# Head pairs transposed together, half-batch loads and a hand-ordered merge in causal attention followed by a SwiGLU feed-forward

## The chip, the cores and the metric

The kernel runs on one core of one Trainium2 chip. The metric is the device time of one execution in microseconds (us). TensorE (PE) multiplies matrices, VectorE (DVE) and ScalarE (ACT) do elementwise work and read the accumulators in PSUM, GpSimd (POOL) does elementwise work in SBUF alone, and SyncE (SP) issues DMAs. Each engine runs its instructions in order and waits on semaphores for the others.

## What is computed

```python
# q, k, v: (8, 8, 576, 64); s: (8, 8, 576)
scores = q @ k.T / 8
cum = np.cumsum(np.maximum(s, 0), axis=-1)
bias = -(cum[..., :, None] - cum[..., None, :])
scores = np.where(causal, -1e9, scores + np.minimum(bias, 0))
attn = softmax(scores) @ v
x = attn.transpose(0, 2, 1, 3).reshape(4608, 512)   # rows: batch, position
g = x @ w_gate                                      # 512 x 1536
out = (g * sigmoid(g) * (x @ w_val)) @ w_out        # 1536 x 512
```

There are 64 heads of 576 positions and 64 dimensions. Inputs and output are float32; both kernels multiply in bf16.

## The kernel before

**Setup.** The running sum of `s` is made for all 64 heads at once by ten shifted additions on DVE (L97 to L103), split into a high and a low bf16 part, and turned by small PE transposes (L124 to L133), so that each head has four extra columns. Appended to the 64 dimensions of q and k, these four columns make the score matmul add the bias.

**Attention.** `load_group` (L135) reads q, k and v of four heads in 15 DMAs whose rows are 256 bytes. `do_head` (L186) casts q and k of one head to bf16 next to the extra columns, turns them with ten PE transposes of 128 columns (L202, five for k and five for q) into `KT` and `QT`, and copies each from PSUM (L205). Scores are made transposed in seven matmuls of 1,920 columns together (L221, the list `SCORE_CHUNKS`), ACT takes the exponential into `Pt` (L230), DVE multiplies each of the five diagonal blocks with a triangle (L239), and fifteen matmuls of 65 columns (L247) give the output and, in the last column, the sum by which L259 divides. The result goes to the DRAM scratch `xdr`.

**Feed-forward.** A tile (`do_moe_tile`, L278) is 512 rows of x. Four DMA transposes (L282) bring it from `xdr`; then for each of 12 column blocks there are four matmuls for the gate `pg` (L292) and four for the value `pv` (L300), a tanh on ACT (L308) and two DVE operations (L310, L314), which give `ht`. 48 matmuls (L320) make the output, ACT or DVE copies it and SP writes it. There are nine tiles.

**Order.** The program names heads, weight pieces and tiles one after another (L333 to L353): after a batch's eight heads come the tiles whose rows earlier batches have finished. A scheduler then orders each engine's instructions, so that in the trace the matmuls of heads and tiles alternate. Pieces of the weights are loaded between groups of heads (`load_weight_piece`, L168) in float32 and cast.

Of the kernel before, what the change touches and what calls it, by code (L numbers as in the profile page):

```python
# [12 lines left out]
FP32 = mybir.dt.float32  # L13
# [6 lines left out]
def kernel(  # L20
# [11 lines left out]
    nc = tc.nc  # L32

    B, H, S, D = q.shape
    BH = B * H
    NT, DM = out.shape
    DF = moe_w_gate.shape[1]

    SP = 640
    NCH = 5  # L40
    AUG = 4
    DEXT = D + AUG
    HGRP = 4

    PT_OFF = []
    o = 0
    for tj in range(NCH):
        PT_OFF.append(o)
        o += SP - 128 * tj
    PT_TOT = o  # L50

    SCORE_CHUNKS = [
        [(0, 0, 512)],
        [(0, 512, 640), (1, 128, 512)],
        [(1, 512, 640), (2, 256, 640)],
        [(3, 384, 640), (4, 512, 640)],
    ]

    const = ctx.enter_context(tc.tile_pool(name="const", bufs=1))
    prep = ctx.enter_context(tc.tile_pool(name="prep", bufs=1))  # L60
    stage = ctx.enter_context(tc.tile_pool(name="stage", bufs=2))
    head = ctx.enter_context(tc.tile_pool(name="head", bufs=4))
    small = ctx.enter_context(tc.tile_pool(name="small", bufs=4))
    wpool = ctx.enter_context(tc.tile_pool(name="wpool", bufs=1))
    moes = ctx.enter_context(tc.tile_pool(name="moes", bufs=4))
    hpool = ctx.enter_context(tc.tile_pool(name="hpool", bufs=3))
    xtp = ctx.enter_context(tc.tile_pool(name="xtp", bufs=8))

    apsum = ctx.enter_context(tc.tile_pool(name="apsum", bufs=1, space=bass.MemoryType.PSUM))
    mpsum = ctx.enter_context(tc.tile_pool(name="mpsum", bufs=4, space=bass.MemoryType.PSUM))  # L70

    dram = ctx.enter_context(tc.tile_pool(name="dram", bufs=1, space=bass.MemoryType.DRAM))

    ident = const.tile([128, 128], BF16)
    make_identity(nc, ident)
    keepmask = const.tile([128, 128], BF16)
    make_upper_triangular(nc, keepmask, val=1.0, diag=True)

    NPT = 4
    ptk_tiles = [const.tile([128, NCH, 128], BF16, name=f"ptk{i}") for i in range(NPT)]  # L80
    ptq_tiles = [const.tile([128, NCH, 128], BF16, name=f"ptq{i}") for i in range(NPT)]
    for t in ptk_tiles + ptq_tiles:
        nc.vector.memset(t[:, :, DEXT:128], 0.0)

    spos = prep.tile([BH, SP], FP32)
    nc.vector.memset(spos[:, S:SP], 0.0)
    s_sb = prep.tile([BH, S], FP32)
    nc.sync.dma_start(s_sb, s.flatten_outer_dims())
# [295 lines left out]
```

## Time and profile before

| | |
|---|---|
| median of 3 runs | 506.57 us (505.91 to 507.78) |
| the profiled execution | span 506.3 us |
| PE busy | 442.4 us (87%), 3,364 matmuls |
| DVE, ACT, POOL busy | 319.3, 298.2, 53.2 us |
[...]
| DMA | 57.44 MB, 46.7% of 16 engines' span |

The span is the time from the first to the last instruction of the profiled execution. "Busy" of an engine counts the time in which at least one of its instructions runs. Matmuls overlap in the pipeline, so a busy PE does not say how many columns it streams: the pace is read from the distance between starts.

### The profile page before, as it was taken

Reading aid. Unit: us, or ns where it says so; the run is one execution under the profiler, and the core shown is the slowest. Engines: PE = TensorE matmul, PEld = TensorE weight load, DVE = VectorE, ACT = ScalarE, POOL = GpSimd, SP = SyncE. Lnnn points to the kernel's source line nnn. Section 1 sums busy time; section 2 is a strip of 40 time slices with the busy share of each in tenths; the row PEclk is TensorE's granted clock in tenths of the full one; section 3 lists DMA queues with packets and bytes.
Section 4 is the critical chain, followed back from the end, with each engine's and each line's share of the span. In section 5 each row is a group of like instructions: output and inputs, shape, how many; then the busy total and the mean of one; then the engine's idle time right before and its main releaser. Section 6 shows DMA issues by size and latency. Waiting matters only on the chain.

```text
span 506.3 us, 10025 instructions
## 1 busy us (share of the span) xinstructions
PE 442.4 (87%) x3364; PEld 237.4 (47%) x3364; DVE 319.3 (63%) x991; ACT 298.2 (59%) x665; POOL 53.2 (11%) x248
## 2 busy tenths in 40 slices
PE   0277743658999999999999999999999999999997
PEld 0144532433445445554555465546554664444443
DVE  8348853645919846983798278828881887174570
ACT  3568865765439527972796289628952984232331
POOL 2013211110001101210121012102100100000000
PEclk9999985969999999999999999999999999999999
DMA  7805779677756751466255715671641121401102
GB/s 167 245 13 123 197 237 170 175 166 182 171 145 144 150 135 49 99 128 161 69 115 126 179 41 116 135 169 41 131 86 65 34 45 34 124 0 37 48 1 83
DMA packets 181124, 57.44 MB, mean 113 GB/s; under 512 B 173840, under 2 KB 173840, under 8 KB 181072
## 3 DMA queue, kind: packets, MB, share of 16 engines
q1 hardware_dynamic: 181072, 56.80, 46.7%
q8 instruction: 26, 0.43, 0.4%
q14 instruction: 26, 0.21, 0.1%
HBM read 37.90 MB, written 14.16 MB: 103 GB/s over the span
## 4 chain that ended last, share of the span: by engine, by line
PE 70%; DMA 10%; ACT 9%; DVE 4%; SPq 4%; issue 2%; ACTq 0%; POOL 0%; DVEq 0%; POOLq 0%
PE py L320 18%; PE pg L292 17%; PE pv L300 16%; PE sc L221 9%; PE tps L202 5%; PE av L247 5%; ACT Pt L230 4%; DMA wld<-in_moe_w_val_dram 3%; DMA wld<-in_moe_w_out_dram 2%; SPq L143 2%; DMA stgq<-in_q_dram 2%; ACT QT L205 1%; DMA stgtq<-in_q_dram 1%; DMA stgk<-in_k_dram 1%; PE htp L127 1%
## 5 line engine op out<-in xcount | busy, mean ns | idle before, releaser
L230 ACT ACTIVATE Pt<-sc 128x512 bf16<-128x512 f32 (+1 forms) x256 | 133.6, 581 | 14.4 <-PE sc L221 12.7
L292 PE MATMUL pg<-xt,wg 128*128 128x512 bf16 x432 | 123.6, 379 | 2.0 <-DMA xt<-xdr 1.5
L300 PE MATMUL pv<-xt,wv 128*128 128x512 bf16 x432 | 120.9, 379 | 0.0
L308 ACT ACTIVATE th<-pg 128x512 bf16<-128x512 f32 x108 | 65.0, 602 | 74.2 <-PE pg L292 69.2
L221 PE MATMUL sc<-QT,KT 128*128 128x128 bf16 (+3 forms) x448 | 87.5, 285 | 11.1 <-ACT QT L205 3.7
L310 DVE SCALAR_TENSOR_TENSOR pp<-th,pg 128x512 bf16<-128x512 bf16 x108 | 73.7, 683 | 35.9 <-ACT th L308 35.5
L320 PE MATMUL py<-wo,ht 128*128 128x512 bf16 x432 | 94.7, 379 | 0.0
L314 DVE TENSOR_TENSOR ht<-pp,pv 128x512 bf16<-128x512 bf16 x108 | 74.1, 686 | 7.8 <-PE pg L292 0.5
L239 DVE TENSOR_TENSOR Pt<-Pt,keepmask 128x128 bf16<-128x128 bf16 x320 | 64.5, 221 | 16.5 <-ACT Pt L230 14.5
L247 PE MATMUL av<-VT,Pt 128*128 128x65 bf16 x960 | 67.9, 198 | 6.9 <-DVE Pt L239 5.5
L328 ACT COPY ysb<-py 128x512 f32<-128x512 f32 x36 | 21.1, 586 | 79.8 <-PE py L320 75.0
L247 PEld LDWEIGHTS <-Pt 128*128 128x128 bf16 x960 | 48.6, 99 | 38.8 <-DVE Pt L239 30.5
L320 PEld LDWEIGHTS <-ht 128*128 128x128 bf16 x432 | 42.2, 98 | 51.0
L221 PEld LDWEIGHTS <-KT 128*128 128x128 bf16 x448 | 42.0, 98 | 50.3 <-issue 34.4
L300 PEld LDWEIGHTS <-wv 128*128 128x128 bf16 x432 | 40.4, 98 | 37.1 <-issue 2.6
L292 PEld LDWEIGHTS <-wg 128*128 128x128 bf16 x432 | 40.7, 98 | 34.9 <-issue 0.9
L197 DVE CAST ptk<-stgk 128x256 bf16<-128x256 f32 x45 | 12.7, 289 | 53.9 <-PE tps L202 48.6
L202 PE MATMUL tps<-ident,ptk 128*128 128x128 bf16 x320 | 31.3, 227 | 13.9 <-ACT ptk L197 13.5
L202 PE MATMUL tps<-ident,ptq 128*128 128x128 bf16 x320 | 35.3, 226 | 2.6 <-ACT KT L205 1.6
L202 PEld LDWEIGHTS <-ptk 128*128 128x128 bf16 x320 | 24.5, 101 | 20.2 <-ACT ptk L197 13.8
L205 DVE COPY KT<-tps 128x640 bf16<-128x640 bf16 x49 | 23.8, 487 | 13.5 <-PE tps L202 13.1
L259 DVE TENSOR_TENSOR ot<-av,recip 128x320 bf16<-128x320 f32 x64 | 31.1, 486 | 0.7 <-DVE Pt L239 0.3
(65 smaller groups left out, 277.2 us busy)
## 6 DMA issues: line engine op xcount, KB each, us to landing
out_dram<-ysb SPq DMA_DIRECT2D x36, 256.0 KB, 2.1
stgq<-in_q_dram SPq DMA_DIRECT2D x64, 128.0 KB, 3.0
stgk<-in_k_dram SPq DMA_DIRECT2D x64, 128.0 KB, 2.9
stgv<-in_v_dram SPq DMA_DIRECT2D x64, 128.0 KB, 2.8
xdr<-ot SPq DMA_DIRECT2D x64, 64.0 KB, 2.3
wld<-in_moe_w_gate_dram SPq DMA_DIRECT2D x4, 768.0 KB, 5.7
wld<-in_moe_w_val_dram SPq DMA_DIRECT2D x4, 768.0 KB, 6.6
wld<-in_moe_w_out_dram SPq DMA_DIRECT2D x12, 256.0 KB, 3.0
```

The source lines that it names most:

```text
L202: nc.tensor.transpose(tps[:, c * 128 : (c + 1) * 128], pt[:, c, :], ident)
L221: nc.tensor.matmul(sc[:, off : off + w], KT[:, 128 * tj : 128 * (tj + 1)], QT[:, ilo:ihi], start=True, stop=True,)
L230: nc.scalar.activation(Pt[:, pt_lo : pt_lo + width], sc[:, 0:width], AF.Exp, scale=0.125,)
L239: nc.vector.tensor_mul(Pt[:, o : o + 128], Pt[:, o : o + 128], keepmask)
L247: nc.tensor.matmul(av[:, bi * (D + 1) : (bi + 1) * (D + 1)], Pt[:, colo : colo + 128], VT[:, tj, :], start=(tj == 0), stop=(tj == bi),)
L259: nc.vector.tensor_mul(ot, av3[:, :, 0:D], recip[:, :, None].to_broadcast([128, NCH, D]),)
L292: nc.tensor.matmul(pg, WG[c][:, ft * 128 : (ft + 1) * 128], xts[c], start=(c == 0), stop=(c == 3),)
L300: nc.tensor.matmul(pv, WV[c][:, ft * 128 : (ft + 1) * 128], xts[c], start=(c == 0), stop=(c == 3),)
L308: nc.scalar.activation(th, pg, AF.Tanh, scale=0.5)
L310: nc.vector.scalar_tensor_tensor(pp, in0=th, scalar=1.0, in1=pg, op0=ALU.add, op1=ALU.mult)
L314: nc.vector.tensor_mul(ht, pp, pv)
L320: nc.tensor.matmul(py, hts[ft][:, ts_ * 128 : (ts_ + 1) * 128], WO[ft], start=(ft == 0), stop=(ft == 11),)
```

## The change

The kernel is written anew around the same arithmetic; the order on every engine is now the order in which the program names the instructions (`manual_schedule`).

- **Loads.** `load_qk` reads q or k of four heads (a half batch) in one DMA with rows of 1,536 bytes (96 partitions of six consecutive positions). `load_v` reads v of a whole batch in five DMAs.
- **Head pairs.** `cast_one` puts two heads side by side in 128 columns. For half batches 0 and 1 `pe_transpose` turns them on PE, six transposes for two heads. From half batch 2 on, `scratch` writes the casted rows to DRAM, `transposes` brings them back with one DMA transpose of 1,152 x 128 for k and one for q, and `split` copies the two 64-row halves on DVE into four standing tiles, whose other rows hold the bias columns (`aug`, a small DMA for each of the four tiles) or zeros (`init_x`).
- **Scores.** Nine matmuls of 1,600 columns together. The four full diagonal blocks are one chunk, which POOL masks with one `affine_select`.
- **First tile.** x of tile 0 is turned on PE out of SBUF (`x_pe`); the others come with one DMA transpose of 512 x 512 (`x_load`) after POOL has issued the write of a whole batch (`x_write`).
- **Merge.** `attn_items` and `ffn_items` yield after each small piece. `pump` advances attention up to a position, in heads; a tile has 36 items, over which eight heads are spread, with fixed offsets (`start`, `LAG`). The weight loads are hooked into it at eight places; their casts are DVE instructions at that place. All weights share two staging buffers.

```diff
-            tps = apsum.tile([128, SP], BF16, tag="tp", bufs=1, name="tps")
-            for c in range(NCH):
-                nc.tensor.transpose(
-                    tps[:, c * 128 : (c + 1) * 128], pt[:, c, :], ident
-                )
-            nc.any.tensor_copy(dstT, tps)
...
-            nc.vector.tensor_mul(
-                Pt[:, o : o + 128], Pt[:, o : o + 128], keepmask
-            )
...
-            next_stg = load_group((gi + 1) // GPB, (gi + 1) % GPB)
-        for h in range(g * HGRP, (g + 1) * HGRP):
-            do_head(b, h, stg)
-        nw = 1 if gi == 0 else 3
-        for _ in range(nw):
-            if wpiece < NWPIECE:
-                load_weight_piece(wpiece)
-                wpiece += 1
-        if g == GPB - 1:
-            while (moe_done + 1) * TT <= b * S:
-                do_moe_tile(moe_done)
-                moe_done += 1
...
+    CHUNKS = [
+        [(0, 0, 128), (1, 128, 256), (2, 256, 384), (3, 384, 512)],
+        [(0, 128, 576), (3, 512, 576)],
+        [(1, 256, 576), (2, 384, 576)],
+        [(4, 512, 576)],
+    ]
...
+    scp = ctx.enter_context(tc.tile_pool(name="scp", bufs=3, space=PSUM))
+    avp = ctx.enter_context(tc.tile_pool(name="avp", bufs=1, space=PSUM))
+    mp = ctx.enter_context(tc.tile_pool(name="mp", bufs=4, space=PSUM))
...
+    with tc.manual_schedule():
...
+        def load_qk(hb):
+            b, g = divmod(hb, 2)
+            for name, src in (("k", k), ("q", q)):
+                t = raw.tile([NP, HB, J, D], FP32, tag="raw" + name, name="raw" + name)
+                nc.sync.dma_start(
+                    t,
+                    src[b, g * HB : (g + 1) * HB, :, :].rearrange(
+                        "h (p j) d -> p h (j d)", j=J
+                    ),
+                )
+                loaded[name, hb] = t
...
+        def init_x(i, eng):
+            for T in (KX[i], QX[i]):
+                eng.memset(T[0][64:128, :], 0.0)
+                eng.memset(T[0][64:68, :], 1.0)
+                eng.memset(T[1][0:64, :], 0.0)
+                eng.memset(T[1][0:4, :], 1.0)
+            for e in range(2):
+                eng.memset(KX[i][e][64 * e : 64 * e + 64, NR * S :], 0.0)
+
+        init_x(0, nc.gpsimd)
...
+        def aug(hb, eng):
+            for T, k0 in ((KX, 0), (QX, 2)):
+                for e in range(2):
+                    r0 = 64 * (1 - e) + k0
+                    eng.dma_start(
+                        T[hb % 2][e][r0 : r0 + 2, 0 : NR * S].rearrange(
+                            "a (r s) -> a r s", r=NR
+                        ),
+                        AUG[hb * HB : (hb + 1) * HB, k0 : k0 + 2, :].rearrange(
+                            "(r e) a s -> e a r s", e=2
+                        )[e],
+                    )
...
+        def cast_one(hb, name, r, eng):
+            if r == 0:
+                cts[name, hb] = cp.tile([NP, NR, J, 2, D], BF16, tag="c" + name, bufs=1, name="c" + name)
+            eng.tensor_copy(
+                cts[name, hb][:, r].rearrange("p j e d -> p e j d"),
+                loaded[name, hb][:, 2 * r : 2 * r + 2, :, :],
+            )
...
+        def scratch(hb):
+            for name, SC in (("k", KS), ("q", QS)):
+                nc.sync.dma_start(
+                    SC[hb].rearrange("(r p j) c -> p r (j c)", r=NR, j=J),
+                    cts[name, hb].rearrange("p r j e d -> p r (j e d)"),
+                )
...
+        def transposes(hb):
+            for name, SC in (("k", KS), ("q", QS)):
+                prs[name, hb] = cp.tile([128, NR * S], BF16, tag="p" + name, bufs=1, name="p" + name)
+                nc.sync.dma_start_transpose(prs[name, hb], SC[hb])
+
+        def split(hb, name, eng):
+            T = {"k": KX, "q": QX}[name][hb % 2]
+            for e in range(2):
+                eng.tensor_copy(
+                    T[e][64 * e : 64 * e + 64, 0 : NR * S],
+                    prs[name, hb][64 * e : 64 * e + 64, :],
+                )
...
+            for j in range(J):
+                nc.tensor.transpose(
+                    ps[:, j, :], ct[:, r, j].rearrange("p e d -> p (e d)"), ident[0:NP, 0:NP]
+                )
...
+            if ci == 0:
+                nc.gpsimd.affine_select(
+                    pt[:, 1088:1600], pt[:, 1088:1600], pattern=[[0, 4], [1, 128]],
+                    compare_op=ALU.is_ge, fill=zreg, base=0, channel_multiplier=-1,
+                )
...
+        def x_write(b):
+            ot = ots[b]
+            nc.gpsimd.dma_start(xdr[b * S + 512 : (b + 1) * S, :], ot[0:TAIL, 4, :])
+            if b > 0:
+                nc.gpsimd.dma_start(
+                    xdr[b * S : b * S + 512, :].rearrange("(c p) e -> p c e", p=128),
+                    ot[:, 0:4, :],
+                )
+
+        def x_load(tt):
+            xts[tt] = xtp.tile([128, 4, TT], BF16, tag="xt", name="xt")
+            nc.sync.dma_start_transpose(xts[tt], xdr[tt * TT : (tt + 1) * TT, :])
...
+                nc.tensor.transpose(
+                    ps[:, c * 128 : (c + 1) * 128],
+                    ots[0][:, c, r * 128 : (r + 1) * 128],
+                    ident,
+                )
+            nc.vector.tensor_copy(xts[0][:, r, :], ps)
...
+            if hb + 1 < NHB:
+                if step == 0:
+                    aug(hb + 1, nc.sync)
+                    if hb + 2 < NHB:
+                        load_qk(hb + 2)
+                    cast_one(hb + 1, "k", 0, nc.gpsimd)
+                    cast_one(hb + 1, "k", 1, nc.gpsimd)
+                if step == 1:
+                    cast_one(hb + 1, "q", 0, nc.gpsimd)
+                    cast_one(hb + 1, "q", 1, nc.gpsimd)
+                    scratch(hb + 1)
+                    if hb % 2 == 0 and hb + 2 < NHB and hb > 0:
+                        load_v((hb + 2) // 2)
+                if step == 2:
+                    transposes(hb + 1)
+                    if hb % 2 == 1:
+                        for c in (0, 1):
+                            cast_v((hb + 1) // 2, c, nc.gpsimd)
+                if step == 3:
+                    split(hb + 1, "k", nc.vector)
+                    split(hb + 1, "q", nc.vector)
+                    if hb % 2 == 1:
+                        for c in (2, 3, 4):
+                            cast_v((hb + 1) // 2, c, nc.gpsimd)
...
+        def attn_items():
+            for bh in range(BH + 2):
+                if bh < BH:
+                    for ci in range(4):
+                        score_piece(bh, ci)
+                        if ci == 1:
+                            side(bh // HB, bh % HB)
+                        yield bh + ci / 8
+                p = bh - 1
+                if 0 <= p < BH:
+                    av_piece(p, (0, 1, 2))
+                    yield bh + 0.5
+                    av_piece(p, (3,))
+                    yield bh + 0.65
+                    av_piece(p, (4,))
+                    av_out(p)
+                    if p % H == H - 1:
+                        x_write(p // H)
+                    if p < H and p % 2 == 0 and p > 0:
+                        x_pe(p // 2 - 1)
+                    yield bh + 0.8
+                    if p == H - 1:
+                        x_pe(3)
+                if bh > H + 1 and (bh - 2) % H == H - 1:
+                    x_load((bh - 2) // H)
+                    yield bh + 0.9
...
+            for ft in range(NFT):
+                j, f0 = divmod(ft * 128, WCH)
+                pg = mp.tile([128, TT], FP32, tag="m", name="pg")
...
+        for nm in ("k", "q"):
+            cast_one(0, nm, 0, nc.vector)
+            cast_one(0, nm, 1, nc.vector)
+        aug(0, nc.scalar)
+        for nm in ("k", "q"):
+            pe_transpose(0, nm, 0, (nc.vector, nc.scalar))
+        for nm in ("k", "q"):
+            pe_transpose(0, nm, 1, (nc.vector, nc.vector))
+        nc.gpsimd.memset(VT[0][:, :, :, D : D + 1], 1.0)
+        nc.gpsimd.memset(VT[0][64:128, 4, :, 0:D], 0.0)
+        for c in range(5):
+            cast_v(0, c, nc.gpsimd)
+        init_x(1, nc.gpsimd)
+        aug(1, nc.sync)
+        nc.gpsimd.memset(VT[1][:, :, :, D : D + 1], 1.0)
+        nc.gpsimd.memset(VT[1][64:128, 4, :, 0:D], 0.0)
...
+        wq = [lambda j=j: load_wgv(j) for j in range(NWCH)] + [
+            lambda j=j: load_wo(j) for j in range(4)
+        ]
+        start = H + 1.2
+        for i in range(8):
+            pump(start * (i + 1) / 8)
+            if i % 2 == 1:
+                wq.pop(0)()
+        for tt in range(NTT):
+            lo = start if tt == 0 else H * (tt + 1) + LAG
+            hi = min(H * (tt + 2) + LAG, BH + 1)
+            span = 36 if tt < 6 else 25
+            n = 0
+            for _ in ffn_items(tt):
+                n += 1
+                pump(lo + (hi - lo) * min(1.0, n / span))
+                if wq and n % 5 == 1:
+                    wq.pop(0)()
+                if tt == NTT - 2 and n == 20:
+                    x_load(NTT - 1)
+        pump(1e9)
```

How the order moves, at three places. The first is SP's queue where before a feed-forward tile's x comes in; `stgk`, `stgq`, `stgv` are loads of a later group, `out_dram` writes results of the tile that runs.

```order
L143 DMA stgv<-in_v_dram 128x4x64 x3
L329 DMA out_dram<-ysb 128x512
L153 DMA stgtv<-in_v_dram 64x4x64
L282 DMA_TRANSPOSE xt<-xdr 128x512
L329 DMA out_dram<-ysb 128x512
L282 DMA_TRANSPOSE xt<-xdr 128x512 x3
L143 DMA stgk<-in_k_dram 128x4x64
```

The same place of the change, for tile 2; `ks`, `qs` are the scratch writes of the next half batch, `pk`, `pq` its transposes.

```order
L180 DMA ks_103<-ck 96x2x768
L180 DMA qs_119<-cq 96x2x768
L120 DMA rawv<-in_v_dram 128x8x64 x4
L125 DMA rawvt<-in_v_dram 64x8x64
L452 DMA out_dram<-ysb 128x512
L331 DMA_TRANSPOSE xt<-xdr 128x4x512
L190 DMA_TRANSPOSE pk<-ks_103 128x1152
L190 DMA_TRANSPOSE pq<-qs_119 128x1152
```

Between the scratch writes and the transposes that read them now stand five loads of v, a result and the transpose of the next tile's x.

The second place is SP's queue where the last gate and value weights are loaded (`wld`). Before:

```order
L172 DMA wld<-in_moe_w_gate_dram 128x1536
L175 DMA wld_878<-in_moe_w_val_dram 128x1536
L143 DMA stgq<-in_q_dram 128x4x64
L172 DMA wld<-in_moe_w_gate_dram 128x1536
L175 DMA wld_884<-in_moe_w_val_dram 128x1536
L143 DMA stgq<-in_q_dram 128x4x64 x3
```

After, where `augd` stands for the bias columns:

```order
L159 DMA q_149<-augd 2x2x576
L109 DMA rawk<-in_k_dram 96x4x384
L109 DMA rawq<-in_q_dram 96x4x384
L180 DMA ks_99<-ck 96x2x768
L180 DMA qs_115<-cq 96x2x768
L120 DMA rawv<-in_v_dram 128x8x64 x4
L125 DMA rawvt<-in_v_dram 64x8x64
L227 DMA wld<-in_moe_w_gate_dram 128x4x384
L227 DMA wld<-in_moe_w_val_dram 128x4x384
L227 DMA wld<-in_moe_w_out_dram 128x3x512
L190 DMA_TRANSPOSE pk<-ks_99 128x1152
```

Before, one load of q stood between the last two pairs; now the fourth pair stands behind the bias columns and scratch writes of half batch 3, the loads of half batch 4 and of v.

The third place is DVE after the change, from the cast of the third pair of weights to the first tile's `pp` and `ht`; `rc` and `ot` are the division of one head, `xps` the first tile's x.

```order
L229 CAST wv_136<-wld 128x1536
L195 COPY k_142<-pk 64x1152
L195 COPY k_143<-pk 64x1152
L195 COPY q_146<-pq 64x1152
L195 COPY q_147<-pq 64x1152
L312 RECIPROCAL rc<-av 128x5
L313 TENSOR_TENSOR ot<-av,rc 128x5x64
L343 COPY xt<-xps 128x512
```

```order
L229 CAST wg_133<-wld 128x1536
L229 CAST wv_137<-wld 128x1536
L426 SCALAR_TENSOR_TENSOR pp<-th,pg 128x512
L231 TENSOR_SCALAR wo_138<-wld 128x1536
L437 TENSOR_TENSOR ht<-pp,pv 128x512
```

The weight casts now stand ahead of the copies that the next scores need and ahead of the first tile's work; before, the scheduler had put them among the heads' masks.

## Rows read from the trace of the kernel before

**Rows 1.** The page: 40 slices of the span (12.66 us each).

```profile
PE   0277743658999999999999999999999999999997
PEclk9999985969999999999999999999999999999999
GB/s 167 245 13 123 197 237 170 175 166 182 171 145 144 150 135 49 99 128 161 69 115 126 179 41 116 135 169 41 131 86 65 34 45 34 124 0 37 48 1 83
```

**Rows 2.** The chain that ended last: start us, us, what.

```profile
57.30 6.34 DMA wld<-in_moe_w_val_dram
...
182.44 10.36 PE py L320 x48
...
231.92 10.36 PE py L320 x48
```

**Rows 3.** Timeline of PE: start us, us, line, form, count.

```profile
199.01 0.44 PE L202 MATMUL tps<-ident,ptk 128*128 128x128 bf16 x5
199.29 0.59 PE L300 MATMUL pv<-xt,wv 128*128 128x512 bf16 x2
...
205.60 0.35 PE L247 MATMUL av<-VT,Pt 128*128 128x65 bf16 x6
205.79 0.38 PE L221 MATMUL sc<-QT,KT 128*128 128x128 bf16 x2
206.01 0.39 PE L202 MATMUL tps<-ident,ptk 128*128 128x128 bf16 x4
```

**Rows 4.** Groups by line and form: busy us, mean ns, idle before.

```profile
L230 ACT ACTIVATE Pt<-sc 128x512 bf16<-128x512 f32 x192 | 108.7, 606 | 14.2 <-PE sc L221 12.6 <-DVE recip L258 1.3
L314 DVE TENSOR_TENSOR ht<-pp,pv 128x512 bf16<-128x512 bf16 x108 | 74.1, 686 | 7.8 <-PE pg L292 0.5
...
L259 DVE TENSOR_TENSOR ot<-av,recip 128x320 bf16<-128x320 f32 x64 | 31.1, 486 | 0.7 <-DVE Pt L239 0.3
...
L173 DVE CAST wg<-wld 128x1536 bf16<-128x1536 f32 x3 | 2.9, 954 | 0.3 <-DMA wld<-in_moe_w_gate_dram 0.3
...
L101 DVE COPY cum_a<-cum_b 64x512 f32<-64x512 f32 x1 | 0.4, 414 | 0.0
```

**Rows 5.** Groups of POOL, same columns.

```profile
L199 POOL COPY ptq<-HTQ 128x20 bf16<-128x20 bf16 x64 | 16.7, 264 | 91.6 <-PE tps L202 84.6 <-ACT HTQ L128 5.3 <-DVE VT L209 1.4
...
L152 POOL MEMSET stgtv<- 64x256 f32 x16 | 5.1, 316 | 9.6 <-ACT VT L210 5.2 <-DVE VT L210 3.5 <-POOL VT L211 0.8
...
masks.py:199 POOL TENSOR_SCALAR_AFFINE_SELECT ident<-ident 128x128 bf16<-128x128 bf16 x1 | 0.3, 294 | 0.0
...
masks.py:197 POOL MEMSET ident<- 128x128 bf16 x1 | 0.2, 205 | 0.3 <-POOLq L368 0.3
```

**Rows 6.** SP's queue in order of time: start us, us of issuing, count.

```profile
176.39 2.20 SPq L143 DMA_DIRECT2D stgv<-in_v_dram  x4
...
179.40 5.14 SPq L282 DMA_TRANSPOSE xt<-xdr  x4
```

**Rows 7.** The tile xt: its DMAs, from the start of the issue.

```profile
DMA to landing us min/median/max: 2.4/2.7/4.3
```

**Rows 8.** All engines in two stretches; the last columns are PEclk, DMA share, GB/s.

```profile
6.00:10.00 4.00, 0.00 (x0) 0.00 (x0) 3.60 (x10) 2.44 (x10) 0.31 (x1) 1.00 0.92 207
57.00:64.00 7.00, 5.57 (x74) 3.85 (x72) 5.39 (x20) 6.31 (x14) 1.47 (x7) 1.00 0.93 289
```

**Rows 9.** PE in stretches: us, busy (instructions), granted clock, DMA share, GB/s.

```profile
64.00:72.00 8.00, 4.23 (x54) 1.00 0.77 258
...
74.00:82.00 8.00, 0.00 (x0) 0.50 1.19 254
82.00:90.00 8.00, 5.70 (x45) 0.52 0.72 147
90.00:95.00 5.00, 4.26 (x51) 1.00 0.38 82
```

**Rows 10.** Timeline of the end: ACT.

```profile
502.64 0.59 ACT L328 COPY ysb<-py 128x512 f32<-128x512 f32 x1 [2.00 <-PE py L320]
```

More of the change, by code (lines that the diff above doesn't have):

```diff
@@ L10 @@
 from concourse._compat import with_exitstack
-from concourse.masks import make_identity, make_upper_triangular
+from concourse.masks import make_identity
 FP32 = mybir.dt.float32
@@ L32 @@
     nc = tc.nc
+    PSUM = bass.MemoryType.PSUM
     B, H, S, D = q.shape
-    BH = B * H
     NT, DM = out.shape
     DF = moe_w_gate.shape[1]
-    SP = 640
+    BH = B * H
     NCH = 5
[L41 to L56, printed above, removed]
-    ]
@@ L59 @@
-    const = ctx.enter_context(tc.tile_pool(name="const", bufs=1))
[L60 to L65, printed above, removed]
-    hpool = ctx.enter_context(tc.tile_pool(name="hpool", bufs=3))
@@ L79 @@
[L79 to L88, printed above, removed]
-    nc.scalar.activation(spos[:, 0:S], s_sb, AF.Relu)
@@ L122 @@
[L122 to L141 removed]
+    TAIL = S - 512
@@ new lines, in score_piece, with av_piece @@
+            if ci == 3:
+                nc.gpsimd.affine_select(
+                    pt[:, 1024:1088], pt[:, 1024:1088], pattern=[[1, 64]],
+                    compare_op=ALU.is_ge, fill=zreg, base=0, channel_multiplier=-1,
+                )
+        avs = {}
+        def av_piece(bh, bis):
+            b, h = divmod(bh, H)
+            if bis[0] == 0:
+                avs[bh] = avp.tile([128, NCH * (D + 1)], FP32, tag="av", name="av")
+            av = avs[bh]
+            pt = pts[bh]
+            for bi in bis:
+                for tj in range(bi + 1):
+                    c0 = pt_col(tj, bi)
+                    nc.tensor.matmul(
+                        av[:, bi * (D + 1) : (bi + 1) * (D + 1)],
+                        pt[:, c0 : c0 + 128],
+                        VT[b % 2][:, tj, h, :],
+                        start=(tj == 0),
+                        stop=(tj == bi),
+                    )
@@ L244, in do_head @@
-        for bi in range(NCH):
-            for tj in range(bi + 1):
-                colo = PT_OFF[tj] + 128 * (bi - tj)
-                nc.tensor.matmul(
-                    av[:, bi * (D + 1) : (bi + 1) * (D + 1)],
-                    Pt[:, colo : colo + 128],
-                    VT[:, tj, :],
-                    start=(tj == 0),
-                    stop=(tj == bi),
-                )
-        av3 = av.rearrange("p (c e) -> p c e", e=D + 1)
-        recip = small.tile([128, NCH], FP32, tag="recip", name="recip")
```

400 lines of the change are left out of this document (200 added, 200 removed).

## The prediction, made before the changed kernel was run

> **What bounds the kernel now.** I read the page's slices first, then the chain of waits, the timeline of PE, and the groups of the other engines. From slice 10 on PE is busy at the full clock nearly all the time; before that it is not, and the DMA moves up to 245 GB/s in the same slices [rows 1]. So the span has two parts: some 125 us in which heads are made and weights come in, with loads of weights on the chain of waits [rows 2], and 380 us in which PE's own work ends last.
>
> The pace in the second part: 48 matmuls of 512 columns take 10.36 us [rows 2], 0.216 each. Five transposes of 128 columns start within 0.28 us (199.01 to 199.29), 0.056 each; six AV matmuls within 0.19, 0.032 each; score matmuls of 128 and 384 columns together take 0.22 [rows 3], so a column costs 0.42 ns. A tile has 144 matmuls, 31.1 us. A head has scores 0.81 (1,920 columns), transposes 0.56 and AV 0.48, together 1.85. One tile and eight heads make 45.9 us; a round of the trace takes 49.48 (182.44 to 231.92) [rows 2]. So 3.6 us a round are lost to small waits. In all PE has 9 x 31.1 + 64 x 1.85 = 398 us of work.
>
> **What goes.** A head's scores shrink to 1,600 columns in nine matmuls, 0.69 us; its transposes leave PE, apart from 48 of 96 columns (0.042 each, 2 us) and 16 of 128 (0.9). A head is then 1.17 us, a round 31.1 + 9.4 = 40.5, and all of PE's work 280 + 75 + 3 = 358: 40 us less, all of it in the part where PE is the bound. The triangle multiplications and the half of the PSUM copies that DVE made go too; PE was busy without a pause beside them, so I count nothing for them.
>
> **What is added in a round.** DVE gets four copies of 64 x 1152 a half batch. A float32 copy of 64 x 512 takes 0.414 and the cast of 128 x 1536 0.954 [rows 4], so one costs between 0.4 and 0.8; the four make 1.6 to 3.2 us. In the 27 us in which a tile's gates and values are made, DVE has 24 operations of 0.686 [rows 4] or about that, 16.4, some five heads at about 0.7 (the division takes 0.486 [rows 4], the reciprocal less) and twice those copies, 23 to 26 us: it fits, just. ACT has 8 x 2.07 (three exponentials of 0.606 [rows 4] and a short one) and sixteen operations of about the same length for the feed-forward, 26.5 of 40.5. I keep the old loss of small waits at 3 us a round for the six rounds after tile 0, 18 us in all.
>
> **The start of each tile.** This is the first new wait. A tile's x comes as one DMA transpose that stands in SP's queue behind the scratch write of q, five loads of v and a result. I count from the moment the round reaches its second batch (head 8m). Heads pass at 5 us each; POOL masks head 8m+1 at about 7.5 us and then casts q. No cast of that size is in the trace: a copy of 20 columns takes 0.264 and a select of 128 columns 0.294 [rows 5], so one of 768 columns lies between 0.26 and 1.76; a memset of 256 columns takes 0.316, and three times that is 0.95. I take 1.1, nearest to it. Two casts end at about 10.5. SP then needs 0.55 for the write, 2.8 for five loads of v (2.20 for four [rows 6]) and 0.4 for the result: the transpose is issued at 14.4. Its issue costs between 1.3 (one DMA of 512 x 128 takes 5.14/4 [rows 6]) and 5.1 (four times as much data); the landing adds 1.4 (2.7 less the issue [rows 7]). And 1.18 MB of v are ahead of it, 5.7 us at 207 GB/s [rows 8]. So x lands between 17 and 21.5; PE is there at 14.6 (36 items of 0.864 + 0.26). PE waits 2.5 to 7 us. Behind it the transposes of the next half batch are issued late by the same amount, each 1.3 to 2.9; DVE stands at the copies between `pp` and `ht` of the first block, and `ht` is late by up to 2 us more. I take 5 us a start; tiles 1 to 6 have it (tile 7's x is fetched while attention has ended), so 30 us, with bounds of 15 and 46.
>
> [...]
>
> **The start of the kernel.** The second new wait, and the larger one. Here the order on SP and DVE decides, and I follow it.
>
> - POOL sets the four standing tiles of both parities with 16 memsets of some 1,200 columns. From 0.205 at 128 columns to 0.316 at 256 [rows 5] that is 1.1 each, 17.6 together; with five casts of v, the first mask comes at about 24 us. SP's bias columns for half batch 1 wait for the same memsets, and the first pair of weights stands behind them: issued at 24, 1.57 MB at 289 GB/s [rows 8] land at 31.
> - The second pair waits for the staging buffer, and the q, k and v of 3.5 MB ahead of it take 12 us: cast at 48. Behind it stand two DMA transposes; the third pair is cast at 60.
> - The copies for head 8 stand behind that cast on DVE. Heads 8 and 9 then run at 2.07 us each, POOL casts q, SP issues v and only then the fourth pair: v and weights are another 11 us, and the cast ends between 74 and 88. I take 80. Ahead of `pp` of tile 0 DVE waits for this cast, so tile 0 starts at 80.
> - From there tile 0's round is 40.5, less 3.5 for the four blocks that PE makes while DVE waits. The third and fourth piece of the output weights stand behind work of heads 12 and 13 and are cast three items later at most, so DVE waits about 7 us for each, and PE, with PSUM for two blocks, 4: 8 us.
> - PE was idle before 80. [...]
>
> So tile 0 ends at 80 + 37 + 8 + 4 = 129.
>
> **The sum.** 129, then six tiles in rounds and two alone: 8 x 31.1 = 249 and the 45 heads from 18.9 on, 53; small waits 18; starts 30; and 4 for the last copy and write (the last copy starts at 502.64 of 506.3 [rows 10]). That is 483 us, against the profiled execution's span of 506.3. The median of the runs lies 0.3 above the span, so the forecast is **483**.
>
> **The rivals.**
>
> - *The waits are short.* Casts near 0.5 us and a transpose whose issue hardly grows with its size: starts cost 15 (-15), the first tile starts at 74 (-6), the output weights cost 2 (-6). 456 us. For it: nothing in the trace shows that a transpose's issue grows. Against it: the v loads ahead are real bytes. [...] Chance 0.22.
> - *The clock falls at each start; slower than before.* An idle PE is followed by a slow one: in 64 to 72 PE was busy 4.23 of 8 us, and the clock was 0.50 from 74 to 82 and 0.52 from 82 to 90 [rows 9]. If a wait of 5 us at a tile's start has the same effect, about 10 us of each round run at half pace, 5 us a start, 30 for six: 513. It decides against the forecast if five of the six starts do so (24 us are between 483 and 507). Against it: between the waits PE is denser than it was in 64 to 72. [...] Chance 0.20.
> - *The new waits eat all of the gain.* Tile 0 at 88 and starts at 7.5 us: 483 + 8 + 15 = 506. Chance 0.08.
>
> **The numbers.** The forecast has 0.5, and its own range is 465 to 502. The range to hold the time 8 times in 10 reaches to the fast rival's centre less 8, and a little over the slow one's: 448 to 518. A difference of 0.5% (2.5 us) is about what a measurement of this kernel can tell from none. Faster: 0.50 + 0.22 = 0.72; the same: 0.08; slower: 0.20.
>
> **What the changed profile would show.** PE's pace per head (fewer transposes, 1,600 columns) is sure. The first `pp` at 74 to 88 us behind the cast of the fourth value weights; PE waiting for the DMA of `xt` 2.5 to 7 us at six starts; the slices of the clock at 9 between them. If the first matmul of each tile waits under 2 us, the fast rival holds; if the clock shows about 7 tenths in the slice after each start, the slow one. The forecast is wrong altogether if DVE becomes the bound inside a round, or if POOL's casts take over 2 us, since each half batch then comes late.

## The result, and the profile after

| | before | after |
|---|---|---|
| median of the runs | 506.24 us (504.63 to 507.78, 4 runs) | 490.65 us (488.41 to 494.78, 4 runs) |
| profiled execution, span | 506.3 us | 486.5 us |
| PE busy, matmuls | 442.4 us, 3,364 | 379.5 us, 2,844 |
| DVE, ACT, POOL busy | 319.3, 298.2, 53.2 us | 241.8, 200.6, 159.5 us |
| mean granted TensorE clock, as a share of full speed | 0.973 | 0.916 |
| DMA | 57.44 MB | 73.33 MB |

The ratio is 0.970, 95% interval 0.965 to 0.976: faster, by 15.6 us. The forecast was 483. In two experiments below one of the four executions was slower (2,263 us in the first with q and k over PE throughout, 446.75 in the one with the fourth half batch over PE); the ratios leave it out, the medians don't.

The page of the changed kernel, 40 slices of 12.16 us, against [rows 1]:

```profile
PE   0262325296958996899599959995999999999996
PEclk9997577588997999799889988998999999999999
GB/s 177 153 211 202 246 221 154 271 140 223 144 214 195 116 131 233 202 106 140 246 189 97 160 232 198 79 186 229 180 77 110 168 2 5 203 13 45 43 0 88
```

Counted from 0, PE starts full work at slice 8 rather than 10, as tile 0 starts earlier. But where the row of before has only nines, every fourth slice now has a 5 or a 6, and the clock's row dips with it. The waits of PE name both:

```profile
PE pg L419 <- DMA xt<-xdr: 30.7, 6, 6.9
PE av L297 <- DVE ot L313: 20.4, 5, 14.5
...
PE pg L419 <- DVE pp L426: 11.3, 1, 11.3
```

(Us in total, times, longest.) The first row is the start of the tiles, 30.7 us in all. The other two lie before tile 0 is under way: PE stands behind DVE, which stands behind weights. On DVE's timeline (start, us, line, in brackets the idle time before and what ended it) the casts of the four pairs of gate and value weights show it, and the first `pp` of tile 0 behind them:

```profile
33.47 0.96 DVE L229 CAST wg<-wld 128x1536 bf16<-128x1536 f32 x1
...
52.90 0.96 DVE L229 CAST wg<-wld 128x1536 bf16<-128x1536 f32 x1 [12.34 <-DMA wld<-in_moe_w_gate_dram]
...
63.76 0.96 DVE L229 CAST wg<-wld 128x1536 bf16<-128x1536 f32 x1 [3.00 <-DMA wld<-in_moe_w_gate_dram]
...
88.25 0.96 DVE L229 CAST wg<-wld 128x1536 bf16<-128x1536 f32 x1 [13.87 <-DMA wld<-in_moe_w_gate_dram]
90.29 0.96 DVE L229 CAST wv<-wld 128x1536 bf16<-128x1536 f32 x1 [1.08 <-DMA wld<-in_moe_w_val_dram]
91.17 0.68 DVE L426 SCALAR_TENSOR_TENSOR pp<-th,pg 128x512 bf16<-128x512 bf16 x1
```

What is late at a tile's start stands in SP's queue (start, us of issuing). This is tile 1:

```profile
135.92 0.32 SPq L180 DMA_DIRECT2D qs<-cq  x1
136.29 3.94 SPq L120 DMA_DIRECT2D rawv<-in_v_dram  x4
140.27 1.14 SPq L125 DMA_DIRECT2D rawvt<-in_v_dram  x1
141.51 0.57 SPq L452 DMA_DIRECT2D out_dram<-ysb  x1
142.19 3.38 SPq L331 DMA_TRANSPOSE xt<-xdr  x1
...
146.28 1.28 SPq L190 DMA_TRANSPOSE pk<-ks  x1
147.66 1.55 SPq L190 DMA_TRANSPOSE pq<-qs  x1
```

Behind the scratch write of q, the five loads of v take 5.1 us, and only then is x's transpose issued. Windows of PE around that start (us, busy, granted clock, DMA share, GB/s):

```profile
133.00:140.74 7.74, 7.63 (x71) 1.00 0.90 235
140.74:147.63 6.89, 0.00 (x0) 0.81 1.15 233
147.63:151.79 4.16, 4.16 (x12) 0.50 1.00 206
151.79:186.00 34.21, 33.89 (x285) 1.00 0.60 146
```

PE stands idle for 6.89 us, then works 4.16 us at a granted clock of 0.50. Tiles 2 to 5 start alike, with 6.3, 5.6, 6.0 and 5.3 us of wait and 3.2 to 3.7 us at 0.50. At tile 6 no v is left to load, and PE waits 0.6.

### The profile page after: what moved, and what is told of

The parts are those of the page before. It is cut to its first block, busy times and chain, and to the rows that moved or that the text cites. A ratio compares the mean times of both kernels' runs of the same rounds, so it can differ in the third digit from the quotient of the medians.

```text
span 486.5 us, 7669 instructions
## 1 busy us (share of the span) xinstructions
PE 379.5 (78%) x2844; PEld 205.6 (42%) x2896; DVE 241.8 (50%) x438; ACT 200.6 (41%) x406; POOL 159.5 (33%) x273
## 2 busy tenths in 40 slices
DMA packets 118773, 73.33 MB, mean 151 GB/s; under 512 B 89424, under 2 KB 111440, under 8 KB 118736
## 4 chain that ended last, share of the span: by engine, by line
PE 57%; DMA 16%; POOL 11%; SPq 5%; issue 5%; DVE 2%; ACT 1%; another core or an unknown queue 0%; POOLq 0%; ACTq 0%; DVEq 0%
PE pv L432 18%; PE pg L419 18%; PE py L443 11%; DMA xt<-xdr 7%; PE sc L264 6%; PE av L297 4%; SPq L120 3%; DMA wld<-in_moe_w_out_dram 3%; DMA rawq<-in_q_dram 3%; DMA wld<-in_moe_w_val_dram 2%; POOL cq L173 2%; POOL pt L276 1%; DMA wld<-in_moe_w_gate_dram 1%; DMA xdr<-ot 1%; POOL ck L173 1%
## 5 line engine op out<-in xcount | busy, mean ns | idle before, releaser
L272 ACT ACTIVATE pt<-sc 128x512 bf16<-128x512 f32 (+1 forms) x256 | 118.7, 503 | 88.8 <-PE sc L264 88.3
L419 PE MATMUL pg<-xt,wg 128*128 128x512 bf16 x412 | 115.7, 398 | 43.3 <-DMA xt<-xdr 30.7
L276 POOL TENSOR_SCALAR_AFFINE_SELECT pt<-pt 128x512 bf16<-128x512 bf16 x64 | 41.6, 649 | 166.5 <-ACT pt L272 166.3
L264 PE MATMUL sc<-q,k 128*128 128x128 bf16 (+4 forms) x576 | 79.2, 255 | 18.2 <-DMA q<-augd 8.6
L437 DVE TENSOR_TENSOR ht<-pp,pv 128x512 bf16<-128x512 bf16 x108 | 74.1, 686 | 10.1 <-PE pv L432 1.2
L264 PEld LDWEIGHTS <-k 128*128 128x128 bf16 x576 | 49.6, 104 | 57.4 <-POOL q L138 8.8
L297 PE MATMUL av<-vt,pt 128*128 128x65 bf16 x960 | 51.5, 198 | 22.1 <-DVE ot L313 20.4
L297 PEld LDWEIGHTS <-pt 128*128 128x128 bf16 x960 | 45.9, 101 | 49.7 <-issue 24.3
L313 DVE TENSOR_TENSOR ot<-av,rc 128x320 bf16<-128x320 f32 x64 | 31.4, 491 | 2.2
L173 POOL CAST cq<-rawq 96x768 bf16<-96x768 f32 x30 | 23.9, 826 | 0.0
L173 POOL CAST ck<-rawk 96x768 bf16<-96x768 f32 x30 | 23.9, 825 | 0.0
L221 POOL CAST vt<-rawv 128x512 bf16<-128x512 f32 x32 | 18.7, 617 | 0.1
```

The source lines that it names most:

```text
L173: eng.tensor_copy(cts[name, hb][:, r].rearrange("p j e d -> p e j d"), loaded[name, hb][:, 2 * r : 2 * r + 2, :, :],)
L264: nc.tensor.matmul(sc[:, o : o + w], kt[:, r * S + 128 * tj : r * S + 128 * (tj + 1)], qt[:, r * S + lo : r * S + hi], start=True, stop=True,)
L272: nc.scalar.activation(pt[:, CHUNK_PT[ci] : CHUNK_PT[ci] + o], sc[:, 0:o], AF.Exp, scale=0.125)
L276: nc.gpsimd.affine_select(pt[:, 1088:1600], pt[:, 1088:1600], pattern=[[0, 4], [1, 128]], compare_op=ALU.is_ge, fill=zreg, base=0, channel ...
L297: nc.tensor.matmul(av[:, bi * (D + 1) : (bi + 1) * (D + 1)], pt[:, c0 : c0 + 128], VT[b % 2][:, tj, h, :], start=(tj == 0), stop=(tj == bi),)
L313: nc.vector.tensor_mul(ot[:, :, h * D : (h + 1) * D], av3[:, :, 0:D], rc[:, :, None].to_broadcast([128, NCH, D]),)
```

## The experiments

The theory was that the order of one queue, SP's, causes both waits: v's loads stand ahead of x and ahead of weights. The rivals were the transposing transfer itself, POOL's casts, and DVE or PE as a bound inside the rounds. Unless said otherwise an experiment edits the changed kernel (490.65 us, 0.970). Times are medians; ratios, with their 95% interval, are to the kernel before.

**v's loads behind the transposes.**

```diff
                 if step == 1:
...
-                    if hb % 2 == 0 and hb + 2 < NHB and hb > 0:
-                        load_v((hb + 2) // 2)
...
                 if step == 3:
                     split(hb + 1, "k", nc.vector)
                     split(hb + 1, "q", nc.vector)
+                    if hb % 2 == 0 and hb + 2 < NHB and hb > 0:
+                        load_v((hb + 2) // 2)
```

> The five loads of v for the next batch are issued one head later, behind the transposes of k and q, instead of ahead of the transpose of x. Theory A (what is late at five tile starts is the issue of x's transpose, because the issues of the five v loads, 3.94 + 1.14 = 5.1 us, stand ahead of it on SP): x's transpose is issued about 5 us earlier, PE's wait for xt falls from about 6.0 us to 0 to 1.5 us at the starts of tiles 1 to 5, the granted clock stays at full there (2.1 us each more), and the kernel takes 5 x (5 + 2.1), about 35 us, less than the changed kernel: about 455 us, ratio to the kernel before 0.90. Rival B (the scratch writes and the transposing transfer itself take the time, whatever is queued ahead): waits stay at 4 us or more and the time falls by less than 10 us (480 to 490). Rival C: v arrives too late for its casts at the next batch, and a new wait of POOL or PE for v takes back what was gained (475 to 490).

Measured: 457.19 us, 0.902 (0.898 to 0.906). Theory A in time and place, though waits of 0.9 to 2.5 us are left and the clock stays up at only three of the five starts; no wait for v shows (rival C). SP's queue at tile 1:

```profile
131.67 0.32 SPq L180 DMA_DIRECT2D qs<-cq  x1
132.08 0.40 SPq L452 DMA_DIRECT2D out_dram<-ysb  x1
133.08 3.22 SPq L331 DMA_TRANSPOSE xt<-xdr  x1
...
137.02 1.28 SPq L190 DMA_TRANSPOSE pk<-ks  x1
138.40 1.63 SPq L190 DMA_TRANSPOSE pq<-qs  x1
...
140.71 3.61 SPq L120 DMA_DIRECT2D rawv<-in_v_dram  x4
```

Head 16, the second batch's end, begins its scores at 122.95 here and at 127.21 in the changed kernel. Counted from there, x's transpose is issued after 10.1 us instead of 15.0, and PE's wait falls by the same amount, from 6.89 to 2.02. Over all starts:

```profile
PE pg L419 <- DMA xt<-xdr: 9.8, 6, 2.5
```

At tile 1 the clock stays at 1.00 behind the wait:

```profile
136.49:138.50 2.01, 0.00 (x0) 1.00 1.18 316
138.50:145.00 6.50, 6.50 (x50) 1.00 1.13 225
```

At tiles 3 and 4 (waits of 0.9 and 1.1 us) the matmuls run at the same pace; from 226 to 267 us the mean granted clock is 1.00. At tiles 2 and 5, behind waits of 2.40 and 2.54 us, the clock still falls:

```profile
181.31:185.00 3.69, 3.69 (x14) 0.63 1.03 263
308.75:312.50 3.75, 3.75 (x13) 0.57 1.09 272
```

What that costs is read from equal work. From a tile's first gate matmul to the AV matmuls behind its third block PE needs 3.06 us at full clock (tiles 1 and 3 here), 4.73 and 4.62 at tiles 2 and 5, and 5.09, 4.63, 4.72, 4.59 and 4.84 at the five starts of the changed kernel. So the lower clock costs 1.5 to 2.0 us a start, 8.6 us in the changed kernel.

The span is 30.4 us shorter. From the first `pp` of tile 1 to that of tile 5 (four rounds) 191.6 us became 171.1, 5.1 a round; some 4.1 of it is wait for x. The other 1.0 is about what the clock gives back: it falls at two starts rather than five, which costs 3.2 us rather than 8.6. I had put down 2.1 a round, with no start slow. Another 6.2 us came at the start, which I had not expected: the fourth weight pair no longer stands behind v's loads either, and its cast moves from 88.25 to 82.05. So a total near the expected one (33.5 us, about 35 expected) is partly luck.

**x ahead of v, k and q behind it.**

```diff
                     scratch(hb + 1)
+                    if hb % 2 == 0 and hb >= 4:
+                        x_load(hb // 2 - 1)
                     if hb % 2 == 0 and hb + 2 < NHB and hb > 0:
                         load_v((hb + 2) // 2)
...
-                if bh > H + 1 and (bh - 2) % H == H - 1:
+                if bh > BH and (bh - 2) % H == H - 1:
                     x_load((bh - 2) // H)
```

> x's transpose is issued right behind the scratch writes and ahead of the five v loads; v and then k and q's transposes follow. Theory A (SP's order decides): PE's wait for xt is gone as in the run with v late (0 to 1.5 us), but k and q's transposes now stand behind x's issue (3.3 us) and v's (5.1 us), so that the split copies on DVE and what is queued behind them may come up to 3 us later than in the changed kernel; 460 to 475 us, ratio 0.91 to 0.94. Rival B (the transposing transfer's own length decides): the waits stay above 4 us, 480 to 490.

Measured: 486.94 us, 0.959 (0.955 to 0.962); the time is in rival B's range, but not for rival B's reason. The waits of PE show it:

```profile
PE sc L264 <- DVE q L195: 29.1, 6, 8.7
...
PE pg L421 <- DMA xt<-xdr: 5.3, 5, 2.0
```

The wait for x is 2 us or less, so the transfer itself is not at fault; the wait for the split copies of q, 8.3 us in one place in the changed kernel, is now 29.1 in six. Whatever stands behind v is late, and PE needs both within a few us.

**Tiles one head later.** `LAG = 2.9` becomes `3.9`, nothing else.

> Nothing changes on the queues: each tile from tile 1 on is only ordered one head later against the attention (2.9 heads behind the batch's end becomes 3.9). Theory A (the data of x arrive about 6 us after PE asks for them, and one head of attention, some 5 us with its share of the feed-forward ahead, can be put in between): waits for xt fall from 6.0 to 0 to 1.5 us at five starts, clock stays up, 450 to 465 us, ratio 0.89 to 0.92; the last tile ends with less attention beside it, which may cost a few us (PE only, no wait). Rival B (PE's order shifts the issue of x's transpose as well, since SP waits there for work of the same heads): waits stay, 480 to 495.

Measured: 492.61 us, 0.971 (0.967 to 0.975), no gain: the time is in rival B's range, but its reason (the waits for x stay) is wrong, so both theories missed. The waits for x are gone, yet:

```profile
PE sc L264 <- DVE q L195: 36.3, 6, 8.2
```

PE now reaches the scores of the next half batch before its tile. It stands there 4.4 to 7.8 us at five starts, for copies whose transposes stand behind v and x. Giving PE other work first changes only which of two late things it waits for.

**q and k over PE throughout**, without and with v's loads late.

```diff
                 if step == 1:
...
-                    scratch(hb + 1)
...
                 if step == 2:
-                    transposes(hb + 1)
+                    for nm in ("k", "q"):
+                        pe_transpose(hb + 1, nm, 0, (nc.vector, nc.vector))
...
                 if step == 3:
-                    split(hb + 1, "k", nc.vector)
-                    split(hb + 1, "q", nc.vector)
+                    for nm in ("k", "q"):
+                        pe_transpose(hb + 1, nm, 1, (nc.vector, nc.vector))
```

> Undoes one part of the change: k and q of every half batch go over TensorE in pairs of heads, as those of the first two half batches do, with the copies out of PSUM on DVE; no scratch writes, no transposing transfers and no split copies of q and k. SP's queue then holds only v ahead of x. Theory A (what the path through DRAM buys is PE time; what it costs is SP's queue): PE has 16 x 20 transposes more, some 14 us, and DVE copies of about 0.75 in place of 0.5 us; the waits for xt fall from 6.0 to about 3 us or less, since the scratch writes and their waits are gone; 480 to 500 us, ratio 0.95 to 0.99. Rival B (PSUM's four buffers, shared with the feed-forward, become the bound): 505 to 530 us, slower than before.

> v's loads late, and k and q of every half batch over TensorE as in the run without transposing transfers of q and k. It shows what the path through DRAM buys once SP's queue no longer delays x. Theory A (PE is the bound then, and 320 transposes more cost PE their time, 398.6 - 379.6 = 19 us of busy PE between the two runs): slower than the run with v late alone by 12 to 22 us, 469 to 480, ratio 0.93 to 0.95. Rival B (the transposes fit in PE's idle time, or DVE's copies of 0.75 us do not delay it): within 5 us of 457.

Measured: 487.64 us, 0.961 (0.954 to 0.969), the same as the changed kernel within the intervals, and theory A; and 459.98 us, 0.907 (0.904 to 0.910), against 457.19 with the path through DRAM: theory B for the second. (The expectation's 320 transposes are 336.) In the first run PE waits 2.4 to 4.1 us for x at five starts, though v still stands ahead of it. That points to the scratch writes, which wait for POOL's casts, as another part of the delay in the changed kernel. PE is busy for 398.6 us against 379.5 in the first pair, and for 386.9 against 379.6 in the second, where 55 of 3,232 matmul records are missing. In the rounds of the second pair that shows: the first `pp` of tiles 1 to 5 lie 44.4 us apart against 42.8. But the scratch writes and transposes are missing from the start as well, and the first `pp` of tile 0 comes at 74.4 instead of 85.0. So the path through DRAM buys 1.6 us a round and loses about 10 before tile 0.

**Weights issued one place earlier.**

```diff
+        def w_cast():
+            dst, t, scale = wfly.pop(0)
             if scale is None:
                 nc.vector.tensor_copy(dst, t)
             else:
                 nc.vector.tensor_scalar_mul(dst, t, scale)
+            w_issue()
```

(`w_issue` starts the next piece's load into the staging buffer that the cast has freed; two pieces are issued at the outset.)

> Alone: each weight piece's load is issued as soon as the cast that frees its staging buffer is ordered, one place earlier in the program; casts and all else stay where they are. Theory A (tile 0 is late, first pp at 91.2 us in the changed kernel, because each pair of weight loads is issued on SP behind v's loads or a wait for q's scratch, and DVE then stands idle for it, 12.3 us at the second pair and 13.9 at the fourth): those two idle times and the 7.4 us for the output weights go, first pp at 70 to 78 us, and the kernel takes 13 to 22 us less than the changed one: 468 to 478, ratio 0.925 to 0.945; the five waits for xt stay near 6 us. Rival B (attention itself, the masks on POOL and the chain of half batches, sets the pace up to tile 0): casts come earlier, but tile 0 does not; less than 5 us, 485 to 492.

Measured: 479.67 us, 0.945 (0.940 to 0.949). Theory A, a little short: the first `pp` moves from 91.2 to 75.0, but then DVE stands at the first piece of the output weights, whose load (81.75 on SP) is issued behind the third batch's v again:

```profile
74.97 0.69 DVE L440 SCALAR_TENSOR_TENSOR pp<-th,pg 128x512 bf16<-128x512 bf16 x1 [1.01 <-ACT th L438]
...
88.45 0.96 DVE L244 TENSOR_SCALAR wo<-wld 128x1536 bf16<-128x1536 f32 x1 [12.79 <-DMA wld<-in_moe_w_out_dram]
```

Six of the sixteen us are given back before tile 1. The waits for x stay (31.7 us).

**Both**, then with the second set of `init_x` memsets on DVE (`init_x(1, nc.vector)`).

> Both edits, v's loads late and weight loads early. If the two causes lie one behind the other on the path, the gains add: 457.2 less the 13 to 22 us of theory A for the weights alone, 435 to 445, ratio 0.86 to 0.88. If tile 0 starts earlier but tiles 1 to 7 are tied to attention (their x comes from the batches, whose half batches are fed by SP and POOL), the gain at the start is given back as waits for xt: 448 to 457.

> Both edits, and the second buffer set's memsets (nine, 17.0 to 26.3 us in the changed kernel) are done by DVE instead of POOL. Theory A (POOL's memsets hold back the first masks and so the first weight pair): first mask at about 19 instead of 27 us, everything up to tile 0 some 4 to 8 us earlier than in the run with both edits alone. Rival B (data of the second half batch and its augmented rows come no earlier, or DVE's casts of the first half batches are held up by the memsets): within 3 us of that run.

Measured: 446.41 us, 0.880 (0.877 to 0.884), and 442.04 us, 0.872 (0.868 to 0.875). The gains add: 490.65 less 33.5 less 11.0 is 446.2. The memsets (ten, not nine) gave 4.4 more, at the lower end of theory A; the first mask comes at 23.8 us instead of 26.4 in the run before, and not at 19, since POOL then waits 7.0 us for ACT's exponentials.

**The third half batch over PE, and further ones.** On the last version; `hb < 2` selects the path over PE, `hb < 3` takes the fourth half batch too, and the third run has `LAG = 3.4`.

> On the version with v late, weights early and the second memsets on DVE (442.04 us): the third half batch's q and k, too, go over TensorE, the later ones through DRAM. Theory A (the longest wait left, 16.5 us from 48.6 to 65.1 us, is PE waiting for the split copies of the third half batch, whose scratch writes and transposes stand on SP behind loads at the start): that wait goes, tile 0 starts 6 to 12 us earlier, 430 to 437, ratio 0.85 to 0.86. Rival B (the fourth weight pair or the loads of q and k for that half batch come no earlier): 440 to 443.

> As the run before, with the fourth half batch over TensorE too. Theory A (at the start DMA and SP are the limit, later PE): 0 to 3 us less than with the third alone, since the fourth half batch's scratch writes leave the queue in which the last weights stand; theory B (its 20 transposes of 64 to 128 columns, about 1.2 us of PE, and copies of 0.75 in place of 0.5 us are in a stretch in which PE is full): 1 to 3 us more.

> As the run with the third half batch over TensorE, and each tile from tile 1 on is ordered 0.5 of a head later. Theory A (the 9.7 us that are still waited for xt at five starts, 1 to 2.7 us each, are data a little late, and now that v's loads no longer stand in the queue half a head covers them): 4 to 8 us less than that run. Rival B (what is late is then again the split copies, as in the run that only moved the tiles by a head): the same time within 2 us.

Measured: 438.41 us, 0.866 (0.861 to 0.870); 441.45 us, 0.871 (0.867 to 0.875); 437.05 us, 0.864 (0.861 to 0.867). The first gains 3.6 us, less than theory A said and with intervals that still touch, and tile 0 starts only 1.1 us earlier. Among PE's waits, this one stands in place of the 16.5 us:

```profile
PE sc L278 <- DVE k L216: 10.5, 1, 10.5
```

and DVE, whose copies stand behind a weight cast, idles 8.4 us for the third weight pair, issued on SP at 50.60 behind the second batch's v:

```profile
58.35 0.96 DVE L242 CAST wg<-wld 128x1536 bf16<-128x1536 f32 x1 [8.40 <-DMA wld<-in_moe_w_gate_dram]
```

```profile
35.90 9.29 SPq L120 DMA_DIRECT2D rawv<-in_v_dram  x4
45.28 1.74 SPq L125 DMA_DIRECT2D rawvt<-in_v_dram  x1
...
50.60 0.39 SPq L236 DMA_DIRECT2D wld<-in_moe_w_gate_dram  x1
```

The other two can't be told from it by their intervals, so for neither is the gain or loss of its theory A or B shown. (The fourth half batch's transposes are 24 of 96 columns.) The last has 0.5 us of waits for x instead of 9.0; its tile 1 starts 5.5 us later, and from there to PE's end it takes 5.2 us less. The first and the last are the best versions, about 13.5% below the kernel before.

**The first tile's x through DRAM.** `x_pe` is left out; all of batch 0's x is written, and `x_load(0)` is issued ahead of tile 0.

```diff
-            if b > 0:
-                nc.gpsimd.dma_start(
...
-                if bh > H + 1 and (bh - 2) % H == H - 1:
+                if bh > H and (bh - 2) % H == H - 1:
...
-        start = H + 1.2
+        start = H + 1.9
```

> Undoes the last part of the change alone, on the changed kernel: the first tile's x goes through DRAM and a transposing transfer like all others, and tile 0 is ordered 0.7 of a head later, behind that load's place. Theory A (tile 0 waits for its fourth weight pair, at 91.2 us in the changed kernel, and x on chip is ready long before): x by DRAM is ready at about the same time or hidden, within 4 us of 490.65. Rival B (x's transpose for tile 0 then stands on SP behind the third batch's v loads as the others do, issued 5 us late, with the write ahead of it): tile 0 starts 5 to 10 us later, 495 to 501, ratio 0.98 to 0.99.

Measured: 488.37 us, 0.967 (0.963 to 0.971), no difference: theory A. The first `pp` comes at 90.7 instead of 91.2. PE waits 13.2 us for x at tile 0, in the time in which it waited 11.3 for the weights before. Turning the first tile on chip buys nothing in this kernel, where the fourth weight pair (cast at 87.80 here) is late in any case; with the weights early it wasn't tried.

## Why the prediction was right

The forecast of 483 is 7.7 us under the median and 3.5 under the profiled execution's span; this part uses the span. (The forecast put the median 0.3 us above the span; the profiled execution took 488.75 us, 2.2 above its own.) Its steps:

- **PE's work.** 40 us less, a round of 40.5. Where the waits for x are gone (the run with `LAG = 3.4`), the first `pp` of tiles 1 to 6 lie 41.1 us apart, against 49.5 before. Right. (1,600 columns at 0.42 ns are 0.67 us and not 0.69, which is 0.2 us a round.)
- **DVE and ACT fit in.** The split copies take 0.455 and 0.569 us (0.4 to 0.8 expected), POOL's casts 0.83 (1.1 taken, 0.26 to 1.76). Behind tile 0 the longest wait of PE for anything but x is 0.7 us, so neither DVE nor POOL sets the pace inside a round.
- **The start of each tile.** "I take 5 us a start; tiles 1 to 6 have it, so 30 us." It was 30.1 at five starts and 0.6 at the sixth. Two terms were mis-sized, in opposite directions. v's loads take 5.1 us of SP instead of 2.8; one now has twice the rows of those in [rows 6], which may be why. The casts end at 8.7 us after head 16 instead of 10.5. So the transpose is issued at 15.0 (14.4 forecast, where its terms add up to 14.3), lands at 20.4 (17 to 21.5), and PE is there at 13.5 (14.6). That the issue is so near is therefore partly luck. That it is the place in the queue, and not the transfer, the first two experiments show.
- **The start of the kernel.** The chain was the forecast one, but every link was some us longer: first mask at 27.3 (24), second pair cast from 52.9 (48), third from 63.8 (60), first `pp` at 91.2 (80, at most 88). The fourth pair is issued at 82.84, right behind 5.0 us of v's loads, which wait for the casts of q. This is the term that was mis-sized most, 11 us, and outside its bounds; the runs with v late (85.0) and weights early (75.0) show that the queue's order makes it. Tile 0 itself then took 48.8 us from its first matmul behind that wait to its end, where 37 + 8 + 4 = 49 was forecast; PE is idle for 6.6 of them. The 4, put down for a slow clock, no run shows as a term of its own: in the changed kernel the granted clock was 0.50 from 84 to 100, PE was busy for 5.63 us from 91.9 to 100, and four gate matmuls took 1.86 us there and 1.03 from 101.95 on. (The round of 40.5 that the forecast starts from has eight heads, while the code spreads 9.7 over tile 0, 2 us more.)
- **Small waits.** From the end of tile 0 (140.74) to the span's end are 345.8 us, and the forecast has 354: without the 30.7 of the starts and the 4.2 at the end (last copy and write), 310.9 are left for what was put at 249 + 53 + 18 = 320. So 9 us were left for the 18 of small waits, and the clock's price at the five starts, 8.6 us, is nearly all of that. The small waits were put far too high: where neither x nor the clock holds PE up, a round has 41.1 - 40.5 = 0.6 us of them, not 3.
- **The sum.** 483 + 11.7 (tile 0 ends at 140.7, not 129) - 8.2 = 486.5. The mechanisms, both new waits and where they stand, were right; that the total is within 3.5 us is partly luck, since a start that was put too early and small waits that were put too high nearly cancel.

The rivals. *The waits are short* fell: the issue of x's transpose takes 3.2 us (median of eight), not 1.3. *The clock falls at each start* came true in its condition (five starts do so) and in part in its sign (the clock's row shows 7, 7, 8, 8, 8 at these starts), but not in its price: 3.2 to 4.2 us at 0.50 instead of ten, and 1.5 to 2.0 us a start by the equal work in the first experiment, where five was forecast. *The new waits eat all of the gain* had its first condition (tile 0 at 91.2, past its 88), but not its second (6.0 us at five starts, not 7.5 at six). For the start alone it was near: tile 0 begins 29 us earlier than before (120.2 to 91.2), but with 8 heads done instead of 18; when tile 1 begins, both kernels have one tile and 18 or 19 heads behind them, and the change is only 4.7 us ahead (154.8 to 150.2).

So the change's gain was real PE time, and most of what it could give was lost in one queue: moving v's loads and the weights' issue, with no arithmetic changed, brought 44 us on top of its 15.6. What stays open: how the 8.4 us by which a round got shorter divide among fewer score columns, fewer transposes on PE and the new order, since only the path through DRAM was taken out by itself; and whether the second batch's v could be moved at the start as well, or v's loads issued on another engine's queue, which wasn't tried.

## What to carry to other kernels

When transfers are gathered into fewer, larger ones on one in-order queue, count the issue time of each and ask what stands behind it: here five loads of v, 5.1 us of issuing, first cast 25 us after their issue had ended, delayed the one that PE needed next. Giving the waiting engine other work first didn't help here, where that work's data stood in the same queue (492.61 us with the tiles a head later); move the transfer that is not urgent, behind all that are (457.19 us with v's loads late). And a path that takes work off the bound engine has to be judged apart in the start-up, where it may stand on the bound: here the path through DRAM buys 1.6 us a round and loses about 10 before tile 0.

## What the hardware showed unexpectedly

- The issue time of the same four loads of v was not a constant. Windows of the changed kernel over four of their issues (us, then busy time of PE, PEld, DVE, ACT, POOL, clock, DMA share, GB/s):

```profile
1.79:10.52 8.73, 0.00 (x0) 0.00 (x0) 2.25 (x2) 1.60 (x2) 8.34 (x9) 1.00 1.10 205
29.16:40.47 11.31, 7.31 (x91) 5.93 (x90) 10.40 (x17) 5.29 (x12) 6.76 (x12) 1.00 1.09 280
77.69:81.54 3.85, 2.94 (x28) 1.69 (x26) 0.00 (x0) 2.24 (x5) 0.99 (x3) 1.00 0.95 206
136.29:140.23 3.94, 3.89 (x35) 2.17 (x34) 0.38 (x1) 2.24 (x5) 0.88 (x2) 1.00 0.96 211
```

  Each stretch is one issue of four loads: 8.73 and 11.31 us where the DMA engines are at 1.1, 3.85 and 3.94 at 0.95. That a full DMA holds SP up is suggested by these rows, not shown.
- A transpose of 512 x 512 takes 3.2 us to issue and 5.4 from issue to landing (tile 1, beside other transfers: the DMA share is 1.15 in PE's wait there), 97 GB/s for 524 KB; one of 1,152 x 128 takes 1.3 to issue (median), the same as one of 512 x 128 did [rows 6].
